# Attention in query blocks of 64 over 168 keys each, in place of 128 over 232

## The chip, the cores and the metric

The kernel runs on one core of one Trainium2 chip. TensorE multiplies matrices (PE in the profile; PEld is its loading of weights), VectorE (DVE), ScalarE (ACT) and GpSimd (POOL) work on elements, and SyncE (SP) issues the DMA transfers. Matmul results land in PSUM, which has eight banks of 512 float32 columns in each of 128 partitions; everything else lies in SBUF. The metric is the device time of one execution in microseconds. Before the change the median of three runs is 312.12 us (311.05 to 313.01).

## The reference

Attention for 4 batches of 8 heads, 768 positions and head size 64, then a gated product. Each query sees the 8 global keys at the start of the sequence and the 96 latest keys up to its own. A bias falls linearly with distance, with a slope for each head. Cut to what matters:

```python
scores = scale * np.matmul(q, k.transpose(0, 1, 3, 2))
rel = pos[:, None] - pos[None, :]
is_global = pos[None, :] < n_global                   # 8
is_local = (rel >= 0) & (rel < n_local)               # 96
dist = np.where(is_global & ~is_local, n_local, np.abs(rel))
scores = scores - slopes[h] * dist
scores = np.where(is_global | is_local, scores, -1e9)
a = np.exp(scores - max) ; a = a / (a.sum(-1) + 1e-9)
x = np.matmul(a, v)                                    # heads side by side: (4, 768, 512)
gate = sigmoid(sum over t of conv_w[t] * x shifted by 4 - t rows)   # 5 taps
out = (gate * (x @ w_val)) @ w_out                     # both weights 512 x 512
```

## The kernel before

Attention is cut into 32 groups. A group (`groups`, L146) is a batch, a half of the sequence (384 positions) and a pair of heads; four pairs of one half come one after the other, so the groups with the first half and those with the second alternate in fours. A group has three steps, one for each query block of 128. A step needs, for all its queries, the 96 keys before the block, the 8 global keys and the 128 keys of the block: a window of 232 keys (`WIN`, L47). The first block of the sequence has only its own 128 (`width`, L206); this text calls it a narrow step and the others wide. There are 80 wide and 16 narrow steps.

For each group, `scores` (L440) makes six float32 matmuls on PE, for three blocks and two heads: 128 queries by 232 keys over the head's 64 dimensions. The two heads lie in the lower and upper 64 partitions of q and k. Their results go to four PSUM banks, two steps of a head to a bank (`S_AT`, L56).

For each step and head, `add_bias` (L453) adds the bias on VectorE and takes the row's minimum, `expo` (L463) makes the exponential and its sum on ScalarE, and `norm` (L480) multiplies by the reciprocal of the sum, mostly on GpSimd, on the step's tile `p`. Then `transpose` (L487) turns the two heads' probabilities with the keys on the partitions, in four matmuls for a wide step: for each head the first 104 keys (only the first 104 queries need those) and the other 128. `evac_pt` (L504) copies the 464 columns from PSUM to SBUF as tile `a`. For the whole group, `pv` (L509) multiplies by v, with v as weights: for each wide step and head one matmul of 128 and one of 104 query columns, each head to its own 64 of the 128 partitions of the PSUM tile `x`.

From x come a rounded copy and its remainder (`x_high`, `x_low`), and the five taps of the convolution on VectorE and ScalarE (`conv`, L618), all read from PSUM. When four groups of a half are done, a sigmoid makes the gate; `val` (L678) and `outp` (L698) are the two products by 512 x 512 weights, each as three matmuls of rounded parts. These weights arrive as 64-bit numbers and are converted in the first part of the run on VectorE, ScalarE, GpSimd and PE.

PSUM holds four banks of scores, one for the transposes (`pt`), one for x and two for the gated product (`S_B`, `PT_B`, `X_B`, L18). So the transposes of a step wait until those of the step before are copied out, and PV of a group until the convolution of the group before has read x.

The order on each engine is the program's. It is made by a list scheduler (`Plan`, L61): each operation has a cost on each engine that may run it, a due time in steps (the `U_` numbers) and the operations it waits for, those that free its buffer among them (`ring`, L79). The scheduler hands out operations in the order of their estimated start and due time. From the fifth group on, PV of group g - 2 is followed at once by the scores of group g (L556 to L559). In three early steps `FILLS` puts filler matmuls ahead of the transposes (L491).

All loads are issued by SyncE in order. A group loads its keys (`rk`), queries (`rq`) and v; the host has laid v out by windows, so that one transfer of 256 or 384 KB brings a group's v (`load_v`, L223) into one of four buffers.

Of the kernel before, what the change touches and what calls it, by code (L numbers as in the profile page):

```python
# [17 lines left out]
S_B, PT_B, X_B = 4, 1, 1  # L18
# [20 lines left out]
P = 128  # L39
# [7 lines left out]
WIN = TAIL + NG + P  # L47
# [8 lines left out]
S_AT = {(k, j): (2 * j + k // 2, k % 2) for k in range(3) for j in range(2)}  # L56
# [80 lines left out]
def attention_moe(ctx, tc, qT, kT, kg, vw, v0, v, counts_in, wv, cw, wo, out):  # L137
# [50 lines left out]
    G = slice(CA, CA + NG)  # L188
# [33 lines left out]

    def load_v(g):  # L223
        b, hf, p = groups[g]
        t = tile_of(("v", g), [P, HB, 2, 2, D], F32, "v", V_B)
        if hf == 0:
            nc.sync.dma_start(t[:, 1:], vw[b, p, :, : HB - 1])
        else:
            nc.sync.dma_start(t, vw[b, p, :, HB - 1 :])

    for g, (b, hf, p) in enumerate(groups):
# [5 lines left out]
        if hf == 0:  # L237
# [5 lines left out]
                 plan.ring("v", V_B, key, [("PV", g)]), P * (HB - 1 + hf) * 4 * D * 4)  # L243
# [17 lines left out]
    def iotas(e):  # L261
# [34 lines left out]
    def distances_all(e):  # L296
        ve = nc.vector
        ve.tensor_scalar(out=d1, in0=rel, scalar1=nlf, scalar2=BIG, op0=ALU.is_ge, op1=ALU.mult)
        ve.tensor_add(d1, d1, rel)
        ve.tensor_scalar(out=d1[:, G], in0=m0[:, :NG], scalar1=nlf, scalar2=None, op0=ALU.add)  # L300

# [138 lines left out]
    def scores(g):  # L440

        hf = groups[g][1]
        banks = [tile_of(("s", g, i), [P, 2, P * 2], F32, "s", S_B, psum) for i in range(4)]
        for k, j in [(k, j) for k in range(HB) for j in range(2)]:
            n = width(3 * g + k)
            c0 = base(HB * hf + k) - kcols(hf)[0] - (TAIL if n == WIN else 0)
            r = slice(j * D, (j + 1) * D)
            i, half = S_AT[k, j]
            T["s", g, k, j] = banks[i][:, half]
            nc.tensor.matmul(T["s", g, k, j][:, :n], T["rq", g][r, k * P : (k + 1) * P],  # L450
                             T["rk", g][r, c0 : c0 + n], start=True, stop=True)

    def add_bias(s, j):  # L453
# [5 lines left out]
            out=t[:, :n], in0=T["s", s // HB, s % HB, j][:, :n], in1=bias[:, h, :P] if n == P else bias[:, h, P:],  # L459
# [517 lines left out]
```

## Time and profile before

| | |
|---|---|
| median of three runs | 312.12 us (311.05 to 313.01) |
| span of the profiled execution, first to last instruction | 310.8 us |
| the median over that span | 1.3 us |
| busy: PE, DVE, ACT, POOL | 284.6, 230.3, 227.7, 148.0 us |
| DMA moved | 36.27 MB, mean 117 GB/s |
| instructions | 6886 |

The page gives the profiled execution by its span; no other time of it is known. Times in the profile are microseconds unless marked ns. A group row reads: line, engine, operation, output tile <- input tiles, shapes, count, then busy time and the mean ns of one, then the engine's idle time just before such instructions with what ended it. A float32 matmul shows as two matmul records and two weight loads, a transpose as one of each. Ends of matmuls are modelled, and neighbours overlap in the records, so the mean of one matmul is longer than the pace at which they follow each other. The chain of waits is the work that ended last, followed back from the last instruction; there a matmul's piece lasts until the next one starts, which is the pace.

### The profile page before, as it was taken

Reading aid. Unit: us, or ns where it says so; the run is one execution under the profiler, and the core shown is the slowest. Engines: PE = TensorE matmul, PEld = TensorE weight load, DVE = VectorE, ACT = ScalarE, POOL = GpSimd, SP = SyncE. Lnnn points to the kernel's source line nnn. Section 1 sums busy time; section 2 is a strip of 40 time slices with the busy share of each in tenths; the row PEclk is TensorE's granted clock in tenths of the full one; section 3 lists DMA queues with packets and bytes.
Section 4 is the critical chain, followed back from the end, with each engine's and each line's share of the span. In section 5 each row is a group of like instructions: output and inputs, shape, how many; then the busy total and the mean of one; then the engine's idle time right before and its main releaser. Section 6 shows DMA issues by size and latency. Waiting matters only on the chain.

```text
span 310.8 us, 6886 instructions
## 1 busy us (share of the span) xinstructions
PE 284.6 (92%) x2156; PEld 226.7 (73%) x2156; DVE 230.3 (74%) x819; ACT 227.7 (73%) x634; POOL 148.0 (48%) x333
## 2 busy tenths in 40 slices
PE   6496978898999999999999999999999999999991
PEld 2363746685888678888788787888797778878980
DVE  4778898988778867878685778977797877795200
ACT  3587876977789678978797779787897779865220
POOL 5934557599435635364426541844444433550220
PEclk9689989999999999999999999999999999999997
DMA  6886654302534444423452354224444121001012
GB/s 187 272 285 210 186 180 136 100 31 86 163 126 121 118 147 146 120 86 83 138 157 80 87 177 145 77 88 127 128 145 111 51 91 64 4 0 69 35 44 69
DMA packets 21069, 36.27 MB, mean 117 GB/s; under 512 B 2592, under 2 KB 12832, under 8 KB 21024
## 3 DMA queue, kind: packets, MB, share of 16 engines
q1 hardware_dynamic: 21024, 35.75, 37.4%
q8 instruction: 19, 0.31, 0.5%
q14 instruction: 26, 0.21, 0.2%
HBM read 29.45 MB, written 6.29 MB: 115 GB/s over the span
## 4 chain that ended last, share of the span: by engine, by line
PE 52%; ACT 17%; DVE 15%; POOL 8%; issue 4%; DMA 2%; SPq 0%; POOLq 0%; ACTq 0%
PE o L703 14%; PE val L683 11%; DVE gate L624 6%; PE s L450 6%; ACT p L468 5%; PE x L526 5%; POOL p L483 4%; PE pt L499 4%; PE x L529 4%; PE pt L502 3%; DVE t L458 3%; DVE xl L616 2%; ACT gate L626 2%; POOL bias L309 2%; ACT xh L159 2%
## 5 line engine op out<-in xcount | busy, mean ns | idle before, releaser
L468 ACT ACTIVATE p<-t,mins 128x232 f32<-128x232 f32 (+1 forms) x192 | 90.3, 471 | 18.5 <-DVE mins L458 16.3
L483 POOL TENSOR_SCALAR p<-p,rs 128x232 f32<-128x232 f32 (+1 forms) x177 | 83.5, 484 | 35.3 <-DVE rs L478 25.1
L624 DVE SCALAR_TENSOR_TENSOR gate<-x,cwt,gate 128x384 f32<-128x384 f32 x128 | 78.5, 613 | 2.0 <-ACT xh L159 1.4
L458 DVE CUSTOM_DVE_ANT_0 t<-s,bias 128x232 f32<-128x232 f32 (+1 forms) x192 | 68.6, 373 | 0.1
L475 POOL TENSOR_SCALAR sm<-sm 128x2 f32<-128x2 f32 x93 | 18.5, 199 | 89.8 <-ACT p L468 85.4
L159 ACT COPY a<-pt 128x464 f32<-128x464 f32 (+1 forms) x87 | 44.6, 512 | 20.7 <-PE pt L502 18.5
L683 PE MATMUL val<-xh,wvh 128*128 128x384 f32 x128 | 46.7, 365 | 1.3 <-DVE g L690 0.8
L450 PE MATMUL s<-rk,rq 64*128 64x232 f32 (+1 forms) x384 | 44.0, 362 | 3.7 <-DMA rq<-in_qT 3.7
L683 PE MATMUL val<-xh,wvl 128*128 128x384 f32 x128 | 43.2, 338 | 0.0
L683 PE MATMUL val<-xl,wvh 128*128 128x384 f32 x128 | 43.2, 337 | 0.0
L703 PE MATMUL o<-woh,gh 128*128 128x512 f32 x96 | 41.2, 430 | 1.0 <-DVE g L690 1.0
L703 PE MATMUL o<-wol,gh 128*128 128x512 f32 x96 | 38.0, 396 | 1.4 <-POOL wol L365 1.4
L696 POOL TENSOR_TENSOR gl<-g,gh 128x384 fp32r<-128x384 f32 x30 | 30.5, 1017 | 18.0 <-ACT gh L159 17.2
L450 PEld LDWEIGHTS s<-rk,rq 64*128 64x128 f32 x384 | 32.0, 187 | 9.0 <-DVE rs L478 3.4
L499 PE MATMUL pt<-ident,p 104*128 104x104 f32 x160 | 32.3, 272 | 6.3 <-POOL p L483 4.3
L499 PEld LDWEIGHTS pt<-ident,p 104*128 104x128 f32 x160 | 20.0, 142 | 24.5 <-POOL p L483 12.5
L703 PE MATMUL o<-woh,gl 128*128 128x512 f32 x96 | 37.8, 394 | 0.0
L468 ACT ACTIVATION_READ_ACCUMULATOR p<-t,mins 128x1 f32 x192 | 36.3, 189 | 0.0
L478 DVE RECIPROCAL rs<-sm 128x2 f32<-128x2 f32 x96 | 15.9, 165 | 27.2 <-POOL sm L475 26.0
L526 PE MATMUL x<-a,v 128*64 128x128 f32 x320 | 32.0, 277 | 0.0
L502 PE MATMUL pt<-ident,p 128*128 128x128 f32 x160 | 30.9, 274 | 0.0
L529 PE MATMUL x<-a,v 104*64 104x104 f32 x320 | 28.0, 252 | 0.0
(166 smaller groups left out, 466.5 us busy)
## 6 DMA issues: line engine op xcount, KB each, us to landing
rq<-in_qT SPq DMA_DIRECT2D x32, 192.0 KB, 3.5
v<-in_vw SPq DMA_DIRECT2D x16, 384.0 KB, 3.3
out<-ob SPq DMA_DIRECT2D x24, 256.0 KB, 2.1
v<-in_vw SPq DMA_DIRECT2D x16, 256.0 KB, 2.7
rk<-in_kT SPq DMA_DIRECT2D x16, 252.0 KB, 3.8
rk<-in_kT SPq DMA_DIRECT2D x16, 200.0 KB, 3.4
w<-in_wv SPq DMA_DIRECT2D x4, 512.0 KB, 4.6
w<-in_wo SPq DMA_DIRECT2D x4, 512.0 KB, 3.8
```

The source lines that it names most:

```text
L159: nc.scalar.copy(dst, src)
L450: nc.tensor.matmul(T["s", g, k, j][:, :n], T["rq", g][r, k * P : (k + 1) * P], T["rk", g][r, c0 : c0 + n], start=True, stop=True)
L458: nc.vector.tensor_tensor_reduce(out=t[:, :n], in0=T["s", s // HB, s % HB, j][:, :n], in1=bias[:, h, :P] if n == P else bias[:, h, P:], op ...
L468: nc.scalar.activation(T["p", s][:, j, :n], T["t", s, j][:, :n], AF.Exp, bias=mins[:, s, j : j + 1], scale=-1.0, accum_out=T["sm", s][:, j ...
L483: engine(e).tensor_scalar(out=pr, in0=pr, scalar1=rs, scalar2=1.0, op0=ALU.mult, op1=ALU.mult)
L499: nc.tensor.transpose(pt[:, j * QA : (j + 1) * QA], pr[:QA, j, :P], ident[:QA, :QA])
L502: nc.tensor.transpose(pt[:, c : c + P], pr[:, j, CA:], ident)
L526: nc.tensor.matmul(head(j, P), T["v", g][:, k, j, 1], a[:, 2 * QA + j * P : 2 * QA + (j + 1) * P], start=True, stop=False)
L529: nc.tensor.matmul(head(j, QA), T["v", g][:CA, k, j, 0], a[:CA, j * QA : (j + 1) * QA], start=False, stop=True)
L624: nc.vector.scalar_tensor_tensor(out=gt, in0=src, scalar=w, in1=gt, op0=ALU.mult, op1=ALU.add)
L683: nc.tensor.matmul(T["val", ph, m], (wvh, wvh, wvl)[r][:, c, m * P : (m + 1) * P], (T["xh", g], T["xl", g], T["xh", g])[r], start=(c == 0 ...
L703: nc.tensor.matmul(T["o", ph, k], (T["gh", ph, c], T["gl", ph, c], T["gh", ph, c])[r][:, cols], (woh, woh, wol)[r][:, c], start=(c == 0 an ...
```

## The change

A query block of 128 is handled as two halves of 64. A half needs the 96 keys before it, the 8 global keys and its own 64: 168 keys (`WIN`). Both halves of a block lie in the same 128 partitions as before, so that one bias add, exponential and normalisation still serve a step and head, now over 168 columns; the bias tables are laid out for it. The parts:

- `scores` makes four matmuls for a step, 64 queries by 168 keys for each half and head, each in its own quarter of the PE array (64 rows by 64 columns). A head's three steps lie in one bank; a group takes two banks.
- `p` has a stride of 192 columns for each head, with 24 zero columns, so that the two heads' 384 columns turn in three transposes of 128 x 128. The middle one holds keys of both heads. Five such tiles are allocated once and their blanks cleared once (`blanks`, on VectorE, before the first other work).
- `evac_pt` copies 384 columns.
- `pv` makes four matmuls for each half, of 64 query columns, where a step had four in all. v comes in four slots: two with keys of one head alone, and two for the middle chunk, in which the other head's half of the partitions is zero. These zeros are also cleared once, in four fixed buffers.
- `load_v` issues three transfers in place of one and brings 1.5 times the bytes.
- PSUM: two banks of scores, two for transposes, two for x, two for the gated product.
- The scheduler's costs for all these steps are changed, and its due times are not.

```diff
-S_B, PT_B, X_B = 4, 1, 1
+S_B, PT_B, X_B = 2, 2, 2
...
-WIN = TAIL + NG + P
+HQ = P // 2
+WIN = TAIL + NG + HQ
+STRIDE = 192
+REST = WIN - P
...
-S_AT = {(k, j): (2 * j + k // 2, k % 2) for k in range(3) for j in range(2)}
...
+    def half_rows(hf):
+        return (0, 2 * HB - 2) if hf == 0 else (2 * HB - 2, 2 * NB - 2)
+
     def load_v(g):
         b, hf, p = groups[g]
-        t = tile_of(("v", g), [P, HB, 2, 2, D], F32, "v", V_B)
-        if hf == 0:
-            nc.sync.dma_start(t[:, 1:], vw[b, p, :, : HB - 1])
-        else:
-            nc.sync.dma_start(t, vw[b, p, :, HB - 1 :])
+        lo, hi = half_rows(hf)
+        t = T["v", g]
+        nc.sync.dma_start(t[:, 0:4:3, : hi - lo], vw[b, p, 0:2].rearrange("c k h d -> k c h d")[:, :, lo:hi])
+        for j, half in enumerate(HALVES):
+            nc.sync.dma_start(t[half, 1 + j, : hi - lo], vw[b, p, 2, half, lo:hi])
+
+    vbuf = [one.tile([P, 4, 2 * HB, D], F32, name=f"v{i}") for i in range(V_B)]
+    pbuf = [one.tile([P, 2, STRIDE], F32, name=f"p{i}") for i in range(P_B)]
+
+    def blanks(e):
+        for t in pbuf:
+            nc.vector.memset(t[:, :, WIN:], 0.0)
+        for t in vbuf:
+            for j in range(2):
+                nc.vector.memset(t[HALVES[1 - j], 1 + j], 0.0)
+
+    plan.add(("BLANK",), -101, {DVE: 2.6}, blanks)
+    for g in range(NGRP):
+        T["v", g] = vbuf[g % V_B]
+    for s in range(NSTEP):
+        T["p", s] = pbuf[s % P_B]
...
-        nc.gpsimd.iota(rel, pattern=[[-1, WIN]], base=TAIL, channel_multiplier=1, allow_small_or_imprecise_dtypes=True)
-        nc.gpsimd.affine_select(out=rel[:, :CA], in_=rel[:, :CA], pattern=[[-1, CA]], compare_op=ALU.is_ge, fill=BIG,
-                                base=TAIL, channel_multiplier=1)
-        nc.gpsimd.tensor_copy(rel[:, CA + NG :], rel0[:, OWN_A:])
+        for half, n in zip(HALVES, FIRST):
+            nc.gpsimd.iota(rel[half, : n + NG], pattern=[[-1, n + NG]], base=TAIL, channel_multiplier=1,
+                           allow_small_or_imprecise_dtypes=True)
+        nc.gpsimd.affine_select(out=rel[:HQ, :CA], in_=rel[:HQ, :CA], pattern=[[-1, CA]], compare_op=ALU.is_ge,
+                                fill=BIG, base=TAIL, channel_multiplier=1)
+        for half, n in zip(HALVES, FIRST):
+            nc.gpsimd.tensor_copy(rel[half, n + NG :], rel0[half, OWN_A : OWN_A + WIN - n - NG])
...
-        banks = [tile_of(("s", g, i), [P, 2, P * 2], F32, "s", S_B, psum) for i in range(4)]
-        for k, j in [(k, j) for k in range(HB) for j in range(2)]:
+        banks = [tile_of(("s", g, j), [P, 4 * P], F32, "s", S_B, psum) for j in range(2)]
+        for k in range(HB):
             n = width(3 * g + k)
-            c0 = base(HB * hf + k) - kcols(hf)[0] - (TAIL if n == WIN else 0)
-            r = slice(j * D, (j + 1) * D)
-            i, half = S_AT[k, j]
-            T["s", g, k, j] = banks[i][:, half]
-            nc.tensor.matmul(T["s", g, k, j][:, :n], T["rq", g][r, k * P : (k + 1) * P],
-                             T["rk", g][r, c0 : c0 + n], start=True, stop=True)
+            for j in range(2):
+                T["s", g, k, j] = banks[j][:, k * WIN : k * WIN + n]
+            for i, half in enumerate(HALVES):
+                c0 = base(HB * hf + k) - kcols(hf)[0] - (TAIL - i * HQ if n == WIN else 0)
+                for j in range(2):
+                    r = slice(j * D, (j + 1) * D)
+                    nc.tensor.matmul(T["s", g, k, j][half], T["rq", g][r, k * P + i * HQ : k * P + (i + 1) * HQ],
+                                     T["rk", g][r, c0 : c0 + n], start=True, stop=True)
...
-            out=t[:, :n], in0=T["s", s // HB, s % HB, j][:, :n], in1=bias[:, h, :P] if n == P else bias[:, h, P:],
+            out=t[:, :n], in0=T["s", s // HB, s % HB, j], in1=bias[:, h, :P] if n == P else bias[:, h, P:],
...
-        if width(s) == P:
-            for j in range(2):
-                nc.tensor.transpose(pt[:, j * P : (j + 1) * P], pr[:, j, :P], ident)
-        else:
-            for j in range(2):
-                nc.tensor.transpose(pt[:, j * QA : (j + 1) * QA], pr[:QA, j, :P], ident[:QA, :QA])
-            for j in range(2):
-                c = 2 * QA + j * P
-                nc.tensor.transpose(pt[:, c : c + P], pr[:, j, CA:], ident)
+        flat = pr.rearrange("p j c -> p (j c)")
+        starts = (0, STRIDE) if width(s) == P else (0, P, 2 * P)
+        for i, c in enumerate(starts):
+            nc.tensor.transpose(pt[:, i * P : (i + 1) * P], flat[:, c : c + P], ident)
...
-        n = 2 * P if width(s) == P else 2 * (QA + P)
-        a, pt = tile_of(("a", s), [P, 2 * (QA + P)], F32, "a", A_B), T["pt", s]
+        n = 2 * P if width(s) == P else 3 * P
+        a, pt = tile_of(("a", s), [P, 3 * P], F32, "a", A_B), T["pt", s]
...
             if width(s) == P:
                 for j in range(2):
-                    nc.tensor.matmul(head(j, P), T["v0", g][:, j], a[:, j * P : (j + 1) * P], start=True, stop=True)
+                    nc.tensor.matmul(x[j * D : (j + 1) * D, c0 : c0 + P], T["v0", g][:, j],
+                                     a[:, j * P : (j + 1) * P], start=True, stop=True)
                 continue
-            for c, j in ((1, 0), (1, 1), (0, 1), (0, 0)):
-                if c:
-                    nc.tensor.matmul(head(j, P), T["v", g][:, k, j, 1], a[:, 2 * QA + j * P : 2 * QA + (j + 1) * P],
-                                     start=True, stop=False)
-                else:
-                    nc.tensor.matmul(head(j, QA), T["v", g][:CA, k, j, 0], a[:CA, j * QA : (j + 1) * QA],
-                                     start=False, stop=True)
-
-    SCORES, SWITCH = 0.39, 0.19
+            v, first = T["v", g], 0 if groups[g][1] else 2
+            for i in range(2):
+                for slot, chunk, j, n in ((0, 0, 0, P), (3, 2, 1, WIN - HQ), (1, 1, 0, P), (2, 1, 1, P)):
+                    nc.tensor.matmul(x[j * D : (j + 1) * D, c0 + i * HQ : c0 + (i + 1) * HQ],
+                                     v[:n, slot, 2 * k + i - first],
+                                     a[:n, chunk * P + i * HQ : chunk * P + (i + 1) * HQ],
+                                     start=chunk != 1, stop=chunk == 1)
+
+    SCORES, SWITCH = 0.285, 0.09
...
-        return deps + ([("AM", 3 * (g - 1) + k, j) for k in range(HB) for j in range(2)] if g else [])
+        h = g - S_B // 2
+        return deps + ([("AM", 3 * h + k, j) for k in range(HB) for j in range(2)] if h >= 0 else [])
...
-    vw = np.ascontiguousarray(vw.transpose(0, 1, 5, 3, 2, 4, 6))
+    win = v[:, :, rows].reshape(B, NP, 2, 2 * NB - 2, WIN, D).transpose(0, 1, 2, 4, 3, 5)
+    vw = np.zeros((B, NP, 3, P, 2 * NB - 2, D), np.float32)
+    vw[:, :, 0] = win[:, :, 0, :P]
+    vw[:, :, 1, : WIN - HQ] = win[:, :, 1, HQ:]
+    vw[:, :, 2, :REST] = win[:, :, 0, P:]
+    vw[:, :, 2, HQ:] = win[:, :, 1, :HQ]
```

More of the change, by code (lines that the diff above doesn't have):

```diff
@@ L186, in attention_moe @@
     hist = one.tile([P, NP, HIST], F32, name="hist")
-    G = slice(CA, CA + NG)
+    HALVES = (slice(0, HQ), slice(HQ, P))
+    FIRST = (CA, CA - HQ)
     T = {}
@@ L299, in distances_all @@
         ve.tensor_add(d1, d1, rel)
-        ve.tensor_scalar(out=d1[:, G], in0=m0[:, :NG], scalar1=nlf, scalar2=None, op0=ALU.add)
+        for half, n in zip(HALVES, FIRST):
+            ve.tensor_scalar(out=d1[half, n : n + NG], in0=m0[half, :NG], scalar1=nlf[half], scalar2=None, op0=ALU.add)
     plan.add(("CNT",), -100, {DVE: 0.6}, read_counts)
@@ L465, in expo @@
         if j == 0:
-            tile_of(("p", s), [P, 2, WIN], F32, "p", P_B)
             tile_of(("sm", s), [P, 2], F32, "sm", 5)
@@ L568, in attention_moe @@
                 key = ("AM", s, j)
-                plan.add(key, due + U_AM, {DVE: 0.32 if full else 0.21}, lambda e, s=s, j=j: add_bias(s, j),
+                plan.add(key, due + U_AM, {DVE: 0.255 if full else 0.21}, lambda e, s=s, j=j: add_bias(s, j),
                          [("S", g), ("BIAS", 2 * groups[g][2] + j, int(full))] + plan.ring("t", T_B, key, [("EX", s, j)]))
@@ L577, in attention_moe @@
                     deps.append(("EX", s, 0))
-                plan.add(key, due + U_EX, {ACT: 0.48 if full else 0.39}, lambda e, s=s, j=j: expo(s, j), deps)
+                plan.add(key, due + U_EX, {ACT: 0.425 if full else 0.39}, lambda e, s=s, j=j: expo(s, j), deps)
             plan.add(("RG", s), due + U_RC - 0.1, {POOL: 0.16, DVE: 0.1}, lambda e, s=s: guard(e, s),
@@ L584, in attention_moe @@
             for j in range(2):
-                plan.add(("NM", s, j), due + U_RC + U_NM, {POOL: 0.46 if full else 0.3, DVE: 0.25 if full else 0.15},
+                plan.add(("NM", s, j), due + U_RC + U_NM, {POOL: 0.36 if full else 0.3, DVE: 0.19 if full else 0.15},
                          lambda e, s=s, j=j: norm(e, s, j), [("RC", s)])
             key = ("PT", s)
-            plan.add(key, due + U_PT, {PE: 0.39 if full else 0.218}, lambda e, s=s: transpose(s),
+            plan.add(key, due + U_PT, {PE: 0.34 if full else 0.23}, lambda e, s=s: transpose(s),
                      [("NM", s, 0), ("NM", s, 1), ("IOTA",)] + plan.ring("pt", PT_B, key, [("EV", s)]))
             key = ("EV", s)
-            plan.add(key, due + U_EV, {ACT: 0.5 if full else 0.3, DVE: 0.58 if full else 0.33},
+            plan.add(key, due + U_EV, {ACT: 0.43 if full else 0.3, DVE: 0.49 if full else 0.33},
                      lambda e, s=s: evac_pt(e, s), [("PT", s)] + plan.ring("a", A_B, key, [("PV", g)]))
@@ L926, in _window_rows @@
         q0 = qb * P
-        first = list(range(q0 - TAIL, q0 + OWN_A))
-        rows.append([first + [q0] * (P - CA), list(range(NG)) + list(range(q0 + OWN_A, q0 + P))])
+        line = list(range(q0 - TAIL, q0 + OWN_A)) + list(range(NG)) + list(range(q0 + OWN_A, q0 + P))
+        rows += [line[i * HQ : i * HQ + WIN] for i in range(2)]
     return rows
```

10 lines of the change are left out of this document (3 added, 7 removed).

## The prediction

> **What bounds the kernel now.** I read the page's summary and slices first, then the busy time by stretches, then the chain of waits, then the groups of instructions with their shapes kept apart, last the DMA issues. The page:
>
> ```profile
> span 310.8 us, 6886 instructions
> PE 284.6 (92%) x2156; PEld 226.7 (73%) x2156; DVE 230.3 (74%) x819; ACT 227.7 (73%) x634; POOL 148.0 (48%) x333
> PE   6496978898999999999999999999999999999991
> ...
> PE 52%; ACT 17%; DVE 15%; POOL 8%; issue 4%; DMA 2%; SPq 0%; POOLq 0%; ACTq 0%
> ```
>
> PE is the busiest engine by 18 points, and from the eleventh slice to the last but one it stands at 9. Since ends of matmuls are modelled, that alone proves little; the stretches and the chain must carry it. Stretches (length, then busy time and count of PE, PEld, DVE, ACT, POOL; clock, DMA share, GB/s), and last the same long stretch with the instructions of the score tile alone (PE, PEld, DVE):
>
> ```profile
> 0.00:10.00 10.00, 5.52 (x25) 2.38 (x27) 5.42 (x26) 4.50 (x13) 6.14 (x25) 1.00 0.73 231
> 10.00:20.00 10.00, 8.05 (x50) 4.94 (x49) 8.10 (x30) 6.05 (x20) 6.61 (x15) 0.66 0.82 270
> 20.00:30.00 10.00, 7.08 (x37) 3.74 (x39) 7.94 (x31) 7.96 (x25) 4.02 (x11) 1.00 0.75 239
> 79.00:259.00 180.00, 176.56 (x1427) 145.33 (x1425) 139.93 (x524) 145.44 (x413) 82.63 (x203) 1.00 0.39 117
> 79.00:259.00 180.00, 29.79 (x264) 21.69 (x264) 47.09 (x132) 1.00 0.39 117
> ```
>
> A group's scores are 12 PE records (each float32 matmul shows as two passes), so 264 of them are 22 groups in 180 us: 8.18 us a group. Now PE's work in a group, from pieces of the chain of waits (start, length, what, records), where PE follows on PE and the length is the pace:
>
> ```profile
> 37.08 0.22 PE pt L496 x2
> 38.20 0.22 PE x L526 x4
> 38.42 0.18 PE x L529 x4
> 48.21 0.18 PE pt L499 x2
> 48.39 0.22 PE pt L502 x2
> 83.79 0.53 PE val L683 x3
> 84.32 0.69 PE o L703 x3
> 135.86 1.38 PE s L450 x12
> 158.60 1.21 PE s L450 x12
> ```
>
> Scores cost 1.38 us in a group of three wide steps and 1.21 in one whose first step has only 128 keys, 1.30 on average. A wide step's transposes cost 0.18 + 0.22 = 0.40 and its PV 0.22 + 0.18 = 0.40; a narrow step costs 0.22 in each. With 2.5 wide and 0.5 narrow steps a group that is 1.11 and 1.11. The gated product has 16 triples of `val` and 12 of `o` for four groups: 4 x 0.53 + 3 x 0.69 = 4.19. Sum 7.71 of 8.18 us, the rest going into changes between kinds of matmul and small waits. So from 79 us on PE's own work is the bound, and the next engine, ACT, is at 145.44 of 180 (81%). Before that it is not: in the first 30 us PE is busy 20.7, with DMA at 73 to 82%.
>
> **The change, part by part.** First the pace. The two score groups differ by 104 columns in two passes of a pair of heads: 0.17 / 208 = 0.82 ns a column and pass. PV's 128 and 104 columns, two passes each (four records, two heads side by side), differ by 0.04: 0.04 / 48 = 0.83. What is left over in a pass of 128 is 0.22 / 2 - 128 x 0.00083 = 0.004 us; in a whole group's scores 1.38 - 6 x 232 x 0.00083 = 0.22 us.
>
> Scores: six tiles of 128 queries become twelve of 64, over 168 columns. The trace shows two row halves side by side in scores and two column halves side by side in PV, never four quarters at once. If the four run together, a wide step is 2 x 168 x 0.00083 = 0.28 us where it was 0.385: -0.32 for three wide steps, -0.21 for two, -0.265 on average. If only two do, it is 0.56; that end is priced as a rival. I take the four, since the trace has each half of it. The weight load that the first pass waits for gets shorter:
>
> ```profile
> L450 PEld LDWEIGHTS s<-rk,rq 64*128 64x128 f32 x384 | 32.0, 187 | 9.0 <-DVE rs L478 3.4 <-DMA rk<-in_kT 1.4 <-issue 0.2
> L526 PEld LDWEIGHTS x<-a,v 128*64 128x64 f32 x320 | 18.3, 136 | 3.3 <-issue 2.2 <-ACT p L468 0.5 <-ACT a L159 0.2
> ```
>
> 187 against 136 ns, so -0.05 a group (between 0 and -0.05). Transposes: a wide step has three of 128 in place of two of 104 and two of 128: 3 x 0.11 = 0.33, -0.07 a step, -0.175 a group. PV: a wide step has eight matmuls of 64 columns where it had four of 128 or 104, in four pairs of two passes: 8 x (64 x 0.00083 + 0.004) = 0.46, +0.06 a step, +0.15 a group. No row has a pass of 64 columns. The low end is the columns alone, 0.425; the high end is the shortest pass that a row shows, that of 104 columns, 0.18 / 2 = 0.09, which makes 0.72. I take 0.46, because the left-over of 0.004 is the same size at 104 and at 128 columns. What makes it tight is the weight load: by the two rows above (51 ns for 64 columns) it takes 51 ns of each 53 ns pass, where it had 87 to 107 ns of cover.
>
> The Trainium skill speaks against this step: its page TensorEngine Tiling (section Instruction Overhead) gives every matmul some 60 cycles of overhead and warns against cutting a dimension that is already small. By it, 60 cycles (25 ns at that skill's 2.4 GHz) on each of eight passes would make the step about 0.63 us, an estimate. The left-over of 4 ns in a pass of 128 does not show such a charge.
>
> Net for PE: -0.265 - 0.05 - 0.175 + 0.15 = -0.34 us a group. It counts in full for the last 24 of 32 groups: -8.2 us.
>
> In the first 79 us, eight groups with 20 wide steps, the other engines matter:
>
> ```profile
> L468 ACT ACTIVATE p<-t,mins 128x232 f32<-128x232 f32 x160 | 77.5, 486 | 9.5 <-DVE mins L458 8.1 <-POOL sm L475 0.4 <-DVE x L605 0.2
> L468 ACT ACTIVATE p<-t,mins 128x128 f32<-128x128 f32 x32 | 12.8, 401 | 9.0 <-DVE mins L458 8.2
> L483 POOL TENSOR_SCALAR p<-p,rs 128x232 f32<-128x232 f32 x145 | 71.1, 502 | 26.9 <-DVE rs L478 19.9 <-PE pt L502 2.6 <-DVE x L605 1.4
> L483 POOL TENSOR_SCALAR p<-p,rs 128x128 f32<-128x128 f32 x32 | 12.4, 400 | 8.4 <-DVE rs L478 5.3 <-DVE x L161 1.5 <-DVE x L605 1.5
> L458 DVE CUSTOM_DVE_ANT_0 t<-s,bias 128x232 f32<-128x232 f32 x160 | 59.8, 391 | 0.1
> L458 DVE CUSTOM_DVE_ANT_0 t<-s,bias 128x128 f32<-128x128 f32 x32 | 8.9, 282 | 0.0
> L159 ACT COPY a<-pt 128x464 f32<-128x464 f32 x74 | 39.9, 539 | 18.7 <-PE pt L502 18.5
> L159 ACT COPY a<-pt 128x256 f32<-128x256 f32 x13 | 4.7, 361 | 2.0 <-PE pt L496 2.0
> ```
>
> Each pair of rows gives a slope; 64 columns less are 52 ns of exponential, 63 of normalisation and 67 of bias add for each head, and 80 columns less of evacuation are 68. A wide step loses 2 x (52 + 63 + 67) + 68 = 432 ns, 20 steps 8.6 us over three engines, of which the path holds one at a time, with DMA and weight conversion between. Bounds 0 and -8.6; I take a quarter, -2.2. Later this is off the path: these engines wait for PE there.
>
> The shared PSUM banks: two score banks instead of four make a group's first score wait for the last bias add of the group before. PE's whole queue stands behind that wait, the gated product too. But no bias add is among what ended PE's idle time before a score (the L450 row above), so nothing; if its cover went, a step's two adds, 0.8 us a group. A second bank for x takes no wait off PV either: its row above shows 3.3 us of idle time in all, mostly issue; 0 to -3.3, taken as 0. A second bank for transposes frees the filler matmuls (L492) of three early steps, which now stand behind an evacuation. These rows (pieces of the chain, a wait, groups, DMA issues and SP's own issue) price the rest:
>
> ```profile
> 0.75 2.96 DMA counts_i<-in_counts
> 20.26 3.58 DMA v<-in_vw
> 44.42 3.79 PE pt L492 x9
> PE pt L492 <- ACT a L159: 3.3, 3, 1.9
> L605 DVE MEMSET x<- 128x4 f32 x16 | 1.0, 62 | 0.0
> L628 DVE TENSOR_SCALAR gate<-x,cwt 128x384 f32<-128x384 f32 x8 | 4.9, 609 | 0.8 <-PE x L529 0.8
> v<-in_vw SPq DMA_DIRECT2D x16, 384.0 KB, 3.3
> v<-in_vw SPq DMA_DIRECT2D x16, 256.0 KB, 2.7
> 151.27 0.33 SPq L227 DMA_DIRECT2D v<-in_vw  x1
> ```
>
> Fillers: 0 to -3.8 (the nine lie on the chain once); I take -1.0, since other early limits come next. New clears on DVE ahead of its first work: five of 2 x 24 and eight of 384 columns. Low: 13 x 62 ns = 0.8 us; high: 8 x 609 + 5 x 62 ns = 5.2. DVE has 2.96 us free while the counts travel, so 0 to +2.2 on the start; I take +0.8, since a clear reads nothing and should lie well under a two-sided pass. Loads of v: 1.5 times the bytes, three issues for one. In groups 0 to 4, loaded while DMA is near full, that is 4 x 128 + 192 KB, 0.72 MB, at 270 GB/s 2.7 us, and ten issues of 0.33 us on SP, behind which the next rk, rq and weights queue. Bounds 0 to +2.7; I take +1.0, as one load alone stands on the early chain. Later DMA is at 39% and takes it in: a v buffer is filled four groups ahead, 33 us, against 3.3 to land.
>
> Sum: -8.2 - 2.2 - 1.0 + 0.8 + 1.0 = -9.6, span 301.2 us. The median of 312.12 lies 1.3 us above the span of 310.8, so 302.5.
>
> **The rivals.** First, the quarters do not run together: the two halves of a score tile go one after the other. A wide step is then 0.56 instead of 0.385 and a narrow one 0.42 instead of 0.21, +0.54 a group in place of -0.265. PE's net becomes +0.47 a group, +11.2 over 24, with the other terms (-1.4) 320.6 of span, 322 us. It decides from 0.20 us for a pass of four (0.14 + 0.34 / 6) upward. For it: no row has four. Against it: either kind of half runs as a pair at full pace.
>
> Second, short PV passes bound by weight loads or by issue. At 0.09 us a pass a wide step is 0.72, +0.65 a group beyond my sum, net +0.31, +7.4 over 24: 318 us. It takes all of the gain from 0.074 us a pass (0.34 / 20 more than 0.057). The skill's rule above would act here, and its 0.63 us a step stands just past that point. For it: the load nearly fills the pass. Against: the left-over of 4 ns.
>
> Third, the gain is lost to order. The list scheduler makes the whole order anew from new costs and banks, while its due times stay those of the old steps; 48% of the chain lies outside PE, in short pieces between PE's. If waits of 0.34 us a group come back, only the other terms are left: 309 to 314. Against: every engine's step gets shorter and no bank gets scarcer in effect.
>
> **How the numbers follow.** My forecast has 0.68, with a range of its own of 296 to 308 (early terms at their ends, -5 to +5). Lost to order 0.12; quarters one after the other 0.08; slow PV passes 0.07; still better, below 296, because the early terms or the freed banks give more, 0.05. The range of 295 to 313 leaves out the two slow cases and some edges. One per cent (309.0 to 315.2) is about what can be told from no change here. Faster by more: 0.68 + 0.05, less the edge of the forecast, plus none of the third: 0.72. Within: 0.12. Slower: 0.16, the two slow cases and the bad edge of the third.
>
> **What would show it.** Scores x24 on the chain at about 1.0 us in a group of three wide steps (1.8 if the quarters run in turn); transposes x3 at 0.33; PV x16 at 0.46 a wide step (0.63 to 0.72 for the second rival); groups 7.84 us apart in the long stretch with PE still at 98%; the first bias add at 7 to 9 us. I am wrong if PE's busy share falls in that stretch while the groups stay 8.2 us apart, or if the start slips by over 3 us.

## The result, and the profile after

| | before | after |
|---|---|---|
| median | 312.56 us (311.05 to 313.02) | 301.22 us (300.91 to 302.3) |
| ratio, with its 95% interval | | 0.9654 (0.9621 to 0.9686) |
| span of the profiled execution | 310.8 us | 299.2 us |
| group 8's first score starts at | 79.5 us | 74.8 us |
| from there to group 31's first score, 23 groups | 188.3 us | 183.4 us |
| from there to the end | 43.1 us | 40.9 us |

The median before is that of the three runs given above and a fourth, so it differs a little from 312.12. The change makes the kernel 3.5% faster. Of the 11.7 us that the span loses (unrounded), 4.6 go before group 8, 4.9 in the 23 groups behind it and 2.2 at the end. The page of the changed kernel: summary, PE's slices, shares of the chain of waits.

```profile
span 299.2 us, 8913 instructions
...
PE 274.5 (92%) x3100; PEld 221.8 (74%) x3100; DVE 212.3 (71%) x815; ACT 217.5 (73%) x647; POOL 141.0 (47%) x340
...
PE   6199799598999999999999999999999999999991
...
PE 58%; ACT 7%; DVE 6%; issue 2%; POOL 2%; ACTq 0%; POOLq 0%
```

Every engine has less to do, PE's share is again 92%, and its slices now show a hole in the second and the eighth. Busy time by stretches, in the columns of the prediction: three stretches of the changed kernel.

```profile
0.00:10.00 10.00, 4.84 (x34) 1.90 (x34) 6.27 (x29) 2.34 (x4) 4.87 (x22) 1.00 0.69 196
10.00:20.00 10.00, 5.81 (x43) 3.43 (x44) 7.66 (x38) 6.72 (x26) 7.29 (x20) 0.66 0.97 302
...
79.00:250.00 171.00, 168.75 (x2043) 140.19 (x2047) 122.30 (x503) 138.24 (x415) 77.50 (x201) 1.00 0.47 143
```

The same long stretch of the kernel before:

```profile
79.00:250.00 171.00, 168.10 (x1364) 138.67 (x1362) 133.53 (x502) 138.18 (x396) 79.57 (x195) 1.00 0.39 117
```

In the first 20 us PE is less busy than before (10.65 us against 13.57) and DMA busier, and yet group 8 starts earlier. In the long stretch PE is busy 98 to 99% in both. Pieces of the chain of waits after the change (start, length, what, records):

```profile
89.54 0.37 PE x L539 x4
89.91 0.93 PE x L545 x32
90.84 0.95 PE s L478 x24
...
131.82 1.55 PE x L545 x48
133.37 1.02 PE s L478 x24
...
135.56 0.33 PE pt L522 x3
```

A group of three wide steps has scores of 1.02 us (1.38 before) and PV of 1.55; one with a narrow step 0.95 (1.21 before) and 0.37 + 0.93. Transposes of a wide step take 0.33. Groups of instructions after the change, different shapes apart:

```profile
L495 ACT ACTIVATE p<-t,mins 128x168 f32<-128x168 f32 x160 | 69.0, 433 | 12.3 <-DVE mins L486 10.7 <-POOL sm L502 0.3 <-DVE x L624 0.2
L510 POOL TENSOR_SCALAR p<-p,rs 128x168 f32<-128x168 f32 x149 | 61.8, 427 | 24.4 <-DVE rs L505 16.6 <-PE pt L522 2.5 <-PE x L545 1.8
L486 DVE CUSTOM_DVE_ANT_0 t<-s,bias 128x168 f32<-128x168 f32 x160 | 49.7, 323 | 0.1
L161 ACT COPY a<-pt 128x384 f32<-128x384 f32 x77 | 36.3, 471 | 8.4 <-PE pt L522 8.1
L478 PE MATMUL s<-rk,rq 64*64 64x168 f32 x640 | 32.1, 318 | 1.8 <-DVE mins L486 1.8
L478 PEld LDWEIGHTS s<-rk,rq 64*64 64x64 f32 x768 | 25.7, 138 | 7.6 <-DVE mins L486 1.7 <-DMA rk<-in_kT 1.4 <-PE pt L522 1.3
```

The exponential of a wide step and head falls by 53 ns, the normalisation by 75, the bias add by 68, the evacuation by 68. Scores now have a wait that they did not have, for a bias add: 1.8 us on PE over the whole run, in three places before group 8 (at 46, 54 and 55 us). The 1.7 on its weight loads are two of the same waits. Last, the start of VectorE on its timeline, after and before:

```profile
1.28 3.85 DVE L245 MEMSET v<- 64x384 f32 x8
5.05 0.10 DVE L306 CAST cf<-counts_i 128x4 f32<-128x4 int32 x1
...
7.85 0.29 DVE L486 CUSTOM_DVE_ANT_0 t<-s,bias 128x128 f32<-128x128 f32 x1
```

```profile
3.73 0.17 DVE L281 CAST cf<-counts_i 128x4 f32<-128x4 int32 x1 [3.73 <-DMA counts_i<-in_counts]
...
6.89 0.27 DVE L458 CUSTOM_DVE_ANT_0 t<-s,bias 128x128 f32<-128x128 f32 x1
```

The clears end 1.3 us after the counts have landed, and the first bias add comes 1.0 us later.

**A reckoning for PE.** Busy PE does not say how much of it is waiting, because the ends of matmuls are modelled. So I worked out from the records what PE does in the 23 groups from group 8 to group 31. Each matmul is given its columns at 0.83 ns (the rounded parts of the gated product at 0.42), counted back from its end less the 0.166 us or so by which a record outlasts its columns (a record of 64 columns is 0.222 us long). What matmuls cover together is "work". The gaps between neighbouring matmuls are sorted by the pair of tiles that the two write (scores, transposes, PV, `val`, `o`). Of each gap, what lies within the lower quartile for its pair is "changeover", and what it has beyond that is "wait". That is a model, good for differences between kernels:

| us in 23 groups | length | work | changeover | wait |
|---|---|---|---|---|
| before | 188.3 | 159.0 | 19.0 | 10.4 |
| after | 183.4 | 155.2 | 18.1 | 10.1 |

By kind, scores go from 25.1 to 19.3, transposes from 24.6 to 21.1, PV from 25.5 to 29.3. The gated product has 1.8 more in this stretch, since more of it falls into it: six matmuls of `o` (1.3 us) that came before group 8, and three of `val` (0.5) that came at the end. The experiments below use the same columns.

### The profile page after: what moved, and what is told of

It is laid out like the page before. It is cut to its first block, busy times and chain, and to the rows that moved or that the text cites. A ratio compares the mean times of both kernels' runs of the same rounds, so it can differ in the third digit from the quotient of the medians.

```text
span 299.2 us, 8913 instructions
## 1 busy us (share of the span) xinstructions
PE 274.5 (92%) x3100; PEld 221.8 (74%) x3100; DVE 212.3 (71%) x815; ACT 217.5 (73%) x647; POOL 141.0 (47%) x340
## 4 chain that ended last, share of the span: by engine, by line
PE 58%; ACT 7%; DVE 6%; issue 2%; POOL 2%; ACTq 0%; POOLq 0%
PE o L722 17%; PE val L702 17%; PE x L545 10%; PE pt L522 7%; PE s L478 5%; DVE gate L643 2%; ACT p L495 2%; PE x L539 1%; DVE xl L635 1%; POOL p L510 1%; ACT gate L645 1%; ACT xh L161 1%; DVE t L486 1%; ACT ob L161 1%; ACT gate L695 0%
## 5 line engine op out<-in xcount | busy, mean ns | idle before, releaser
L495 ACT ACTIVATE p<-t,mins 128x168 f32<-128x168 f32 (+1 forms) x192 | 81.7, 428 | 15.6 <-DVE mins L486 13.6
L510 POOL TENSOR_SCALAR p<-p,rs 128x168 f32<-128x168 f32 (+1 forms) x181 | 74.9, 426 | 31.7 <-DVE rs L505 23.0
L522 PE MATMUL pt<-ident,p 128*128 128x128 f32 x272 | 51.0, 286 | 9.8 <-POOL p L510 9.5
L486 DVE CUSTOM_DVE_ANT_0 t<-s,bias 128x168 f32<-128x168 f32 (+1 forms) x192 | 58.6, 316 | 1.6 <-PE s L478 1.5
L502 POOL TENSOR_SCALAR sm<-sm 128x2 f32<-128x2 f32 x91 | 18.1, 199 | 85.9 <-ACT p L495 81.2
L522 PEld LDWEIGHTS pt<-ident,p 128*128 128x128 f32 x272 | 33.1, 141 | 29.0 <-POOL p L510 19.2
L161 ACT COPY a<-pt 128x384 f32<-128x384 f32 (+1 forms) x91 | 41.4, 455 | 10.4 <-PE pt L522 10.1
L545 PEld LDWEIGHTS x<-a,v 128*64 128x64 f32 (+1 forms) x1280 | 41.7, 140 | 3.7 <-issue 3.6
L545 PE MATMUL x<-a,v 128*64 128x64 f32 (+1 forms) x1280 | 44.4, 225 | 0.0
L478 PE MATMUL s<-rk,rq 64*64 64x168 f32 (+1 forms) x768 | 36.6, 315 | 3.1 <-DVE mins L486 1.8
L505 DVE RECIPROCAL rs<-sm 128x2 f32<-128x2 f32 x96 | 15.5, 162 | 26.2 <-POOL sm L502 25.0
L478 PEld LDWEIGHTS s<-rk,rq 64*64 64x64 f32 x768 | 25.7, 138 | 7.6 <-DVE mins L486 1.7
```

What stands on the lines that cost most here:

```text
L161: nc.scalar.copy(dst, src)
L478: nc.tensor.matmul(T["s", g, k, j][half], T["rq", g][r, k * P + i * HQ : k * P + (i + 1) * HQ], T["rk", g][r, c0 : c0 + n], start=True, st ...
L486: nc.vector.tensor_tensor_reduce(out=t[:, :n], in0=T["s", s // HB, s % HB, j], in1=bias[:, h, :P] if n == P else bias[:, h, P:], op0=ALU.a ...
L495: nc.scalar.activation(T["p", s][:, j, :n], T["t", s, j][:, :n], AF.Exp, bias=mins[:, s, j : j + 1], scale=-1.0, accum_out=T["sm", s][:, j ...
L510: engine(e).tensor_scalar(out=pr, in0=pr, scalar1=rs, scalar2=1.0, op0=ALU.mult, op1=ALU.mult)
L522: nc.tensor.transpose(pt[:, i * P : (i + 1) * P], flat[:, c : c + P], ident)
```

## The experiments

Two theories. **PE's work is the bound**, as the prediction had it: then a microsecond of work added to PE or taken from it moves the time by one, and shorter element work does nothing after the first 79 us. **The order and the chain through the element engines are as much the bound**: then PE's work counts in part, element work counts throughout, and what the scheduler can do with the banks counts most. Every median below was taken beside runs of the kernel before, whose medians lay between 312.6 and 312.9 us.

### Adding work to PE: halves in turn, and a fourth transpose

```diff
-            for i, half in enumerate(HALVES):
+        for i, half in enumerate(HALVES):
+            for k in range(HB):
+                n = width(3 * g + k)
```

> The changed kernel with the score matmuls in another order: all blocks of the first half, then all of the second, so that two quarters of the array work at a time and not four. If PE is the bound and the four quarters ran side by side, a group's scores go from about 1.0 to 1.8 us, +0.8 us in each of the last 24 groups, and this stands at 317 to 322 us. If PE has slack, or the quarters never ran together, it stays below 306 us.

```diff
         for i, c in enumerate(starts):
             nc.tensor.transpose(pt[:, i * P : (i + 1) * P], flat[:, c : c + P], ident)
+        if width(s) != P:
+            nc.tensor.transpose(pt[:, 3 * P :], flat[:, 2 * P :], ident)
```

> The changed kernel with a fourth transpose in each of the 80 wide steps, into the unused quarter of the bank. 0.11 us a step is 0.27 us a group. If PE is the bound from the eighth group on, +6.6 us (24 groups) to +8.8 us (all 80 steps): 307 to 311 us. If the shorter work of the other engines made the gain, PE has room for it and it stays below 304 us.

Halves in turn: 305.51 us, ratio 0.9744 (0.9709 to 0.9778). Fourth transpose: 306.13 us, 0.9765 (0.9731 to 0.9798). From the chain and the stretches of the first, then of the second:

```profile
126.29 1.35 PE s L480 x24
...
79.00:250.00 171.00, 170.34 (x1984) 144.45 (x1983) 121.38 (x500) 135.85 (x413) 78.38 (x202) 1.00 0.46 143
```

```profile
138.21 0.11 PE pt L524
...
79.00:250.00 171.00, 169.98 (x2036) 143.51 (x2035) 121.05 (x496) 135.53 (x411) 78.42 (x203) 1.00 0.47 143
```

| us in 23 groups | length | work | changeover | wait |
|---|---|---|---|---|
| after | 183.4 | 155.2 | 18.1 | 10.1 |
| halves in turn | 185.6 | 162.1 | 18.1 | 5.4 |
| fourth transpose | 186.0 | 161.4 | 18.1 | 6.6 |

The order of the work is the same in all three. In turn, scores cost 1.35 us in place of 1.02, +6.9 us of work in the 23 groups, or 9.6 in all 32 at the same rate; the time rises by 4.3. The fourth transposes are 80 x 0.11 = 8.8 us; the time rises by 4.9. So over the run a microsecond added to PE costs about half of one (0.45 and 0.56 by the medians; the ratios give rises of 2.8 and 3.5 us, that is 0.29 and 0.40). In the 23 groups, where the prediction had PE as the bound and the granted clock stood at 1.00 in all three, the length rises by 2.2 us for 6.9 of work and by 2.6 for 6.2: 0.32 and 0.42. The rest fills waits, which fall from 10.1 to 5.4 and 6.6. PE was not the only bound even at 98.7% busy.

The scores in turn were 1.35 and not twice 0.86 plus a changeover. The starts show two series of pairs, each with passes 0.143 us apart; the second series begins 0.35 us after the first, not at its end. Why, the records don't tell.

### Only the element work shorter

The kernel before, with bias add, exponential and normalisation over 168 of a wide step's 232 columns, in probability tiles allocated once whose other columns are cleared once. This leaves a part of the attention out: the last 64 keys of each wide window count as zero. Matmuls, evacuation, banks and loads are those of the kernel before.

```diff
+    pbuf = [one.tile([P, 2, WIN], F32, name=f"p{i}") for i in range(P_B)]
+    def blanks(e):
+        for t in pbuf:
+            nc.vector.memset(t[:, :, CUT:], 0.0)
+    plan.add(("BLANK",), -101, {DVE: 0.6}, blanks)
...
+        n, full = min(n, CUT), n > P
...
-        n = width(s)
+        n = min(width(s), CUT)
```

> The kernel before with bias add, exponential and normalisation over 168 instead of 232 columns and nothing else changed; the other 64 columns of the probabilities are zeros, so part of the attention is left out. If PE is the bound, only the first groups gain: 309 to 312 us against 312.6. If the shorter work of DVE, ACT and POOL made the gain, 302 to 306 us.

318.46 us, ratio 1.0199 (1.014 to 1.0258): slower, though every element operation had become shorter. The one planned operation `BLANK` had changed the whole order: group 8 started at 84.4 us instead of 79.5. So it was run again with the clears issued ahead of the planned work, which leaves the order of the kernel before, operation by operation:

```diff
-    plan.add(("BLANK",), -101, {DVE: 0.6}, blanks)
...
+        for t in pbuf:
+            nc.vector.memset(t[:, :, CUT:], 0.0)
```

> The kernel before with bias add, exponential and normalisation over 168 columns again (part of the attention left out), but with the blank columns cleared ahead of the plan, so that the order on every engine is that of the kernel before. If the 6 us lost in the first such run came from the new order that one more planned operation made, this stands at 309 to 312.5 us; if shorter element work gains in itself, 302 to 308; if it really costs, 317 or more.

306.37 us, ratio 0.9792 (0.9761 to 0.9823). Its stretches:

```profile
10.00:20.00 10.00, 8.55 (x42) 5.72 (x43) 7.68 (x30) 5.23 (x17) 6.33 (x14) 1.00 0.75 265
...
79.00:250.00 171.00, 168.63 (x1366) 140.74 (x1365) 129.81 (x518) 135.43 (x403) 75.61 (x196) 1.00 0.38 118
```

| us in 23 groups | length | work | changeover | wait | group 8 starts |
|---|---|---|---|---|---|
| before | 188.3 | 159.0 | 19.0 | 10.4 | 79.5 |
| short elements, its own order | 190.9 | 159.4 | 19.1 | 12.4 | 84.4 |
| short elements, the order of before | 185.2 | 159.0 | 18.8 | 7.4 | 76.7 |

With the order held, shorter element work is worth 6.5 us, and 3.1 of the profiled execution's gain fall in the 23 groups after group 8's start, where PE's waits go from 10.4 to 7.4. The two kernels with short elements differ by 12 us, through one planned operation and the order that followed. In this profiled execution part of the early gain may be the clock, which was granted at 1.00 in 10 to 20 us, where the kernel before had 0.66. The 6.5 us of the median do not rest on that: of its four executions, the two with mean clocks of 0.984 and 0.985, within the 0.972 to 0.988 of the runs before, were the faster ones, 305.9 and 305.6 us.

### The change's work in the order of before

The changed kernel with all of the scheduler's old costs and load sizes, one bank for the transposes and one for x (`PT_N` and `X_N` are the banks that the tiles are allocated in), and the clears ahead of the planned work. Its order is that of the kernel before, operation by operation. The second kernel differs in one thing: two banks each are allocated for the transposes and for x, which the order makes no use of, so that only waits at run time can go.

```diff
-S_B, PT_B, X_B = 2, 2, 2
+S_B, PT_B, X_B = 2, 1, 1
+PT_N, X_N = 1, 1
...
-    plan.add(("BLANK",), -101, {DVE: 2.6}, blanks)
...
-    SCORES, SWITCH = 0.285, 0.09
+    SCORES, SWITCH = 0.39, 0.19
...
+        blanks()
```

> All of the changed work (halves of 64, 168 columns, three transposes, eight PV matmuls, new loads), but one bank each for transposes and x, and the scheduler fed with the old costs, so that every engine's order is that of the kernel before; only the clears come ahead. If the shorter work gains when the order stays (shorter element work alone gave 6.5 us so), and PE's 0.3 us a group comes on top of it, 299 to 304 us. If the single banks hold it back at run time, 305 to 309. If the work is worth nothing without another order, 310 or more.

```diff
-PT_N, X_N = 1, 1
+PT_N, X_N = 2, 2
```

> As the run above, still in the old order, but with two banks each for transposes and x allocated. In the order planned for single banks this took 2.5 us off, so 2 to 3 us below the run above. If the second banks matter only through the order, no difference from it.

The first: 308.02 us, ratio 0.9832 (0.9797 to 0.9866). The second: 306.49 us, 0.9809 (0.9769 to 0.9848); the intervals overlap, so the banks at run time are not shown to be worth anything in this order. The first kernel's stretches, and what PE and its weight loads waited for in the long one (in total, times, longest):

```profile
10.00:20.00 10.00, 7.75 (x50) 5.06 (x52) 8.48 (x32) 6.30 (x21) 6.76 (x16) 0.52 1.00 305
...
79.00:250.00 171.00, 166.07 (x1992) 137.08 (x1985) 128.71 (x511) 132.05 (x400) 74.81 (x194) 1.00 0.46 142
```

```profile
PE o L722 <- DVE g L709: 1.8, 3, 0.8
PEld pt L522 <- POOL p L510: 8.4, 29, 0.7
PEld o L722 <- DVE g L709: 2.7, 3, 1.2
PEld val L702 <- DVE g L709: 1.6, 2, 1.0
```

The same waits with short elements in the order of before, and then in the kernel before. There narrow and wide transposes are on lines of their own (L502 and L505, L496 and L499), here all on L522:

```profile
PEld pt L505 <- POOL p L489: 2.7, 10, 0.3
PEld pt L502 <- POOL p L489: 2.3, 10, 0.4
PEld val L689 <- DVE g L696: 1.4, 2, 0.7
```

```profile
PE o L703 <- DVE g L690: 0.7, 2, 0.5
PEld pt L499 <- POOL p L483: 3.8, 13, 0.5
PEld pt L496 <- POOL p L483: 2.8, 11, 0.5
PEld o L703 <- DVE g L690: 1.6, 3, 0.8
PEld val L683 <- DVE g L690: 1.5, 2, 0.7
```

| us in 23 groups | length | work | changeover | wait | group 8 starts |
|---|---|---|---|---|---|
| before | 188.3 | 159.0 | 19.0 | 10.4 | 79.5 |
| short elements, the order of before | 185.2 | 159.0 | 18.8 | 7.4 | 76.7 |
| all the new work, the order of before | 185.2 | 153.1 | 17.8 | 14.3 | 78.5 |
| the same, two banks allocated | 184.2 | 153.1 | 17.8 | 13.2 | 77.8 |

This is the table that decides. PE has 5.9 us less work and 1.0 less changeover than with short elements alone, and the 23 groups are as long, 185.2: all of PE's gain turned into waits. Most of them are waits for normalised probabilities, which go from 5.0 us (2.7 and 2.3) with short elements to 8.4, and for the gated values `g`, which go on the weight loads from 2.6 to 4.3: that is, for the end of the element chain. (The two kernels differ also in the evacuation, which is shorter here, in the score banks, two against four, in the loads of v and in the clears. No score waits for a bias add in this run, and DMA stands at 46% in the stretch.) In the order of before, then, what ends the 23 groups is the element chain and not PE. The reverse, PE's shorter work with the element work of before, was not run.

### The banks

The changed kernel with other numbers of banks, each with the order that the scheduler makes for them, and one with the order for single banks but two allocated (`PT_N`, `X_N`).

```diff
-S_B, PT_B, X_B = 2, 2, 2
+S_B, PT_B, X_B = 2, 1, 1
```

> The changed kernel with two banks of scores as changed, but one bank for transposes and one for x, planned and allocated so. The run with the old shares took 310.5 us, against my forecast. If it was the single banks that cost this, 308 to 312 us again; if it was the order that four score banks let the scheduler make, 301 to 304 us.

```diff
-S_B, PT_B, X_B = 2, 2, 2
+S_B, PT_B, X_B = 2, 1, 1
+PT_N, X_N = 2, 2
```

> The order planned with one bank for transposes and one for x, as in the run above, but two banks of each allocated, so that only waits at run time can change. If the second banks act by taking waits away, 301 to 304 us; if they act by letting the scheduler make another order, within 2 us of the run with one bank each.

```diff
-S_B, PT_B, X_B = 2, 2, 2
+S_B, PT_B, X_B = 2, 2, 1
```

> The changed kernel with two banks for transposes and one for x, planned and allocated so. If the transposes' second bank carries the banks' share, 300 to 304 us; if x's second bank does (convolution reads x for some 5 us before PV may write again), 307 to 312 us; if both count alike, 304 to 307.

```diff
-S_B, PT_B, X_B = 2, 2, 2
+S_B, PT_B, X_B = 2, 1, 2
```

> The changed kernel with one bank for transposes and two for x, planned and allocated so. The second bank for x has taken 7.9 us off where transposes had two. If it works alone, 302 to 304 us; if both banks are needed together, 307 to 311 us.

```diff
-S_B, PT_B, X_B = 2, 2, 2
+S_B, PT_B, X_B = 4, 1, 1
```

> The changed kernel with the old shares of PSUM: four banks of scores, one for transposes, one for x. If the gain is PE's shorter matmuls, the freed banks are worth 0 to 2 us, and this stands at 300 to 304 us. If the second banks for transposes and x made the gain by taking waits away, it stands at 307 us or above.

| banks (scores, transposes, x) | median, us | ratio (95%) | group 8 starts | 23 groups | wait |
|---|---|---|---|---|---|
| 2, 1, 1 | 311.55 | 0.9957 (0.994 to 0.9974) | 80.0 | 190.5 | 13.9 |
| 2, 1, 1 planned, two allocated | 309.01 | 0.9877 (0.9861 to 0.9894) | 78.7 | 189.9 | 13.2 |
| 4, 1, 1 | 310.49 | 0.9925 (0.9902 to 0.9948) | 81.7 | 185.2 | 14.0 |
| 2, 2, 1 | 309.14 | 0.9882 (0.9855 to 0.9908) | 79.8 | 187.2 | 12.3 |
| 2, 1, 2 | 304.26 | 0.972 (0.9692 to 0.9747) | 75.1 | 185.9 | 12.2 |
| 2, 2, 2, the change | 301.22 | 0.9654 (0.9621 to 0.9686) | 74.8 | 183.4 | 10.1 |

With single banks nearly all of the gain is lost: 311.6 us, with every matmul and element operation as short as after. That is within 1% of the kernel before. Two banks at run time alone bring 2.5 us; the order that is made for two brings 7.8 more. x's second bank is worth 7.3 us without the transposes' second bank and 7.9 with it, the transposes' 2.4 and 3.0. So the banks' worth lies mostly in what the scheduler can place where, and most of that is x's. The lengths of the 23 groups are not quite like for like here: in the first two rows 3.5 us more of the gated product falls into them than in the change.

The kernel with the change's work in the order of before (308.0) beats the one with the same work and banks in its own order (311.6). So the new costs, with the clears as a planned operation, led to a worse order than the old ones.

Why the second x bank helps so much is shown only in part. One would expect that with one bank the five taps of the convolution must come at once, since PV of the next group waits behind them, and that with two they can wait. In groups 1 to 7 the traces show this: with one bank PV never starts before the last tap on VectorE of the group before; with two it does in 2 of 7 groups (2, 1, 2) and in 4 of 7 (the change), and group 8 starts 5 us earlier than with single banks. From group 8 to group 30 it does so in 1 of 23, and the taps are done a median of 4.95 to 4.97 us after PV in these two kernels, against 4.95 to 5.42 with one bank. So in the 23 groups it is something else in the order that helps, and what it is stays open.

### The clears off VectorE's start

```diff
-    plan.add(("BLANK",), -101, {DVE: 2.6}, blanks)
...
+        blanks(nc.gpsimd, vbuf[V_B // 2 :])
...
+        for t in pbuf:
+            nc.vector.memset(t[:, :, WIN:], 0.0)
+        blanks(nc.vector, vbuf[: V_B // 2])
```

> The changed kernel, with the clears of the value halves and of the probability margins taken out of the planned work: half of the value clears go to GpSimd behind its index patterns, the other half and the margins stay on VectorE, and the order of the rest is made without them. If the clears delay the start as the trace suggests (VectorE's first count at 5.05 us instead of 3.73, first bias add at 7.85 instead of 6.89), the time falls by about their share, 0.5 to 2 us: 299 to 300.7. If the start hides them behind the transfers, 301.2 within 1. The order differs a little from the changed kernel's, and the earlier runs showed an order alone to be worth up to 12 us; so 303 and above means that the order found without the clears is a worse one, and says nothing of the clears.

The order of the rest, made without the planned clears, is almost that of the changed kernel. 300.76 us (300.4 to 302.05), ratio 0.9626 (0.9605 to 0.9647). VectorE's start on its timeline:

```profile
1.26 1.86 DVE L243 MEMSET v<- 64x384 f32 x4
3.78 0.17 DVE L304 CAST cf<-counts_i 128x4 f32<-128x4 int32 x1 [0.65 <-DMA counts_i<-in_counts]
...
6.85 0.29 DVE L484 CUSTOM_DVE_ANT_0 t<-s,bias 128x128 f32<-128x128 f32 x1
```

The counts are read 1.3 us and the first bias add comes 1.0 us earlier; group 8 starts at 74.1 us instead of 74.8, and the median is 0.5 us lower. The intervals of this kernel and the changed one overlap, so a gain is not shown: their ends allow from 2.5 us less to 0.8 us more (0.9605 against 0.9686, 0.9647 against 0.9621, times 312.8).

## Why the prediction was right, and where it was wrong

The forecast of 302.5 us, a span of 301.2, stands against 301.22 and 299.2. The total is right; its terms are not, and the errors cancelled. That it came out so near is luck.

**PE's pieces: right.** Forecast -0.34 us a group. Measured on the chain: scores -0.36 with three wide steps and -0.26 with a narrow one, -0.31 on average, where the forecast had -0.265 and -0.05 for the first weight load. Over 23 groups, transposes lose 3.5 us of work, 0.15 a group (0.175 forecast), and PV gains 3.8, 0.165 (0.15 forecast); in sum -0.30. The four quarters start within 20 ns of one another, with passes of 168 columns 0.143 us apart; passes of 64 columns are 0.058 us apart (0.93 for 16 pairs of them, in the chain above). So the first and the second rival fall. The Trainium skill's page TensorEngine Tiling (Array Packing) (section Instruction Overhead) gives each matmul about 60 cycles of overhead. Added to the columns, as the prediction read it, a pass of 64 columns would take some 0.078 us, an estimate (0.053 for the columns and 25 ns); the trace does not agree, with 0.058.

**"It counts in full for the last 24 of 32 groups": this step failed.** From group 8's start to the end the span fell by 7.0 us (231.4 to 224.3) against 8.2, which looks like a small miss, but not for the reason given. In the order of before, taking that work off PE shortened the 23 groups by nothing beyond what the element work gave; in the new order, adding such work cost a third to a half of its length. The prediction took 98% busy as proof that PE's own work is the bound. It had itself summed 7.71 of 8.18 us a group and put the other 0.47 down to changes and small waits: those are 10.8 us in 23 groups, more than the 9.6 us that it forecast as the whole gain. The Trainium skill's page Perfetto Trace Analysis (section Identifying the Most-Contended Engine) says that TensorE's busy share is no good measure of how close a kernel is to its roofline, because pipelined instructions look smaller in the trace. The runs agree that the share misleads, though here it is too high: PE is 97% busy in the new work in the order of before, where 14.3 of 185.2 us were waits.

**"Later this is off the path": failed too.** Shorter element work was taken at -2.2, all of it early. Alone, in the order of before, it was worth 6.5 us, 3.1 of them in the 23 groups after group 8's start.

**The banks: mis-sized.** A second bank for x was taken as 0 because its row showed no wait. But an order that is planned around one bank has no waits on it to show: the cost is in where things were put. Measured: 7.3 to 7.9 us. A second bank for transposes was taken at -1.0, measured -2.4 to -3.0. Two score banks instead of four were taken as free; scores now wait 1.8 us in all on bias adds, and with the other banks single, four gave 310.5 and two 311.6, each in an order of its own.

**The start: right in size.** Clears +0.8, bounds 0 and 2.2: VectorE's counts came 1.3 us later, and without that the median is 0.5 lower, which the intervals don't separate. The loads of v, +1.0, were not tried by themselves. DMA is busier in the first 20 us (0.97 of it in 10 to 20 us, where it was 0.82), and a load of 384 KB lands in 3.7 us instead of 3.3:

```profile
v<-in_vw SPq DMA_DIRECT2D x16, 384.0 KB, 3.7
```

Up to group 8 the forecast had -1.4 us in sum; measured were -4.6. Of that, the new work in the order of before brings 1.0, at an early clock that was lower (0.52 in 10 to 20 us, against 0.66 before and after); the rest comes with banks and order, 1.3 of it because `o` matmuls moved behind group 8's start.

**The third rival, the gain lost to order,** was the real danger and had 0.12. The same work with single banks and an order of its own came out at 311.6, inside its 309 to 314. What kept it away was the second x bank, which the prediction had put at nothing. Its argument against, that no bank gets scarcer, was beside the point: the order also depends on the costs and on every operation planned, and with single banks the new ones made an order 3.5 us worse than the old (311.6 against 308.0).

**What would show it.** Scores at 1.02, transposes at 0.33 and the first bias add at 7.85 us came as forecast; PV at 1.55 for three wide steps is 0.52 a step with its changeover, against 0.46 without. Groups are 7.97 us apart (183.4 / 23) against 7.84, with PE at 98.7%. From those lines alone the theory would have seemed confirmed. Only the runs that held the order fixed or added work to PE showed that it was not.

So the path from 312.6 to 301.2 is: the new work in the old order, to 308.0; two banks at run time, to 306.5, not told apart from nothing; the order that two banks allow under the new costs, 5.3 us more. The forecast booked nearly all of it under the first.

## What to carry to other kernels

A TensorE that is busy 98% of the time in the records can still hold waits as long as the gain you look for. So reckon its work and its waits apart, from paces, before you book a saving in full, or add work to it and see: here a microsecond more cost only a third to a half of one. In a kernel whose order is planned, a buffer's worth can't be read from waits, because the plan has placed the work around the shortage; and any new cost or operation makes another order, worth up to 12 us here. Hold the order fixed if you want to know what a change of the work is worth, and then let it go to see what the order adds.

## What the runs showed of the hardware

- Four 64 x 64 matmuls of float32 in the four quarters of the array run side by side at full pace: pairs 0.006 us apart, all four within 20 ns, the next pass 0.143 us later for 168 columns.
- Passes of 64 columns run 0.058 us apart, with a weight load of 64 columns for each. The columns alone are 0.053 at 0.83 ns, so the loads hide almost wholly.
- Scores with the halves in turn took 1.35 us, not the 1.8 of the first rival: the second half's passes began 0.35 us after the first's.
- The clock early on is not the same in all executions: in the profiled ones it was granted in 10 to 20 us at 0.66 before and after, 0.52 in the new work in the order of before and 1.00 with short elements in the same order, whose PE had been busy 7.64 us in the first ten where those had 4.84 to 5.52. It differs within a kernel too: the four executions of the new work in the order of before had mean clocks of 0.973 to 0.996, and took 308.3 and 306.8 us at these two ends.
- Eight clears of 64 x 384 take VectorE 3.85 us: they start 0.50 us apart, though one record is 0.378 us long.
